# A recurrence and its experts on one core: experts in two walks, the first amid the recurrence's last third, weights in slices of 256 units, token rows scattered into slot order

## The chip, the cores and the metric

The kernel runs on one core of a Trainium2 chip. The metric is device time in microseconds (us) of one execution. The engines named below are TensorE (PE), VectorE (DVE), ScalarE (ACT), GpSimd (POOL) and SyncE (SP). PE's weight loads are shown apart (PEld). The clock in the views is the share of full TensorE clock that was granted.

## The reference

A linear recurrence runs over 768 steps for 4 x 8 heads of size 40. Its output, laid out as 3072 tokens of 320 numbers, goes through a mixture of eight experts: each token goes to the expert with the highest gate logit.

```python
for t in range(768):
    y[:, :, t] = einsum('bhd,bhde->bhe', r_t, state)
    Sa = einsum('bhde,bhe->bhd', state, a_t)
    state = state * w_t - einsum('bhd,bhe->bhde', Sa, b_t) + einsum('bhd,bhe->bhde', v_t, k_t)
x = y.transpose(0, 2, 1, 3).reshape(3072, 320)
e_idx = argmax(x @ w_gate); gate_w = softmax(x @ w_gate)[e_idx]
eom = sigmoid(x @ w_output_gate)
for e in range(8):
    h = maximum(x[e_idx == e] @ w1[e], 0)          # 320 -> 1024
    out[e_idx == e] = gate_w * eom[..., e] * (h @ w2[e])   # 1024 -> 320
```

All is float32. The routing must be exact enough to choose the same expert, and the products accurate, so each matmul operand of the experts is split into a high and a low part (hh and hl, w1h and w1l, and so on), and three products are summed.

## The kernel before

**The recurrence.** `Att` cuts the 768 steps into 12 chunks of 64 steps. A chunk has 16 pairs of heads in two halves (q = 0, 1); I call one (chunk, q) a half-chunk. For each chunk `scan` (POOL or DVE) makes running products of the decay w, `prep` makes the matrices LA, KB, WT and N from them (loads of D, PE products pl, ACT copies, POOL masks at L247, PE transposes at L159), and `tinv` inverts triangular 32 x 32 blocks on DVE (L276 to L317) for one or two chunks at a time. N goes through DRAM (Nd, Ns) to be laid out for `tinv`, and the inverse through Td to Tc. `crit` is the serial part of a half-chunk: pa (L370), solves with Tc (L380), a product with N (L407), another solve, XU (L417, L418), and the next state XS through pS (L427 to L437). `tail` makes the output x from it (pM at L463, pY at L480 and L481, x at L483).

`run` interleaves these by hand. The main loop goes through the half-chunks; after each step of `crit` it lets the tail of the half-chunk before take a step, lets the background take RATE = 4 steps, and the routing of finished halves one. The background is `prep` and `tinv` for all later chunks and, at its end, the early part of the experts. So that PE's clock stays up, `fill` issues dummy matmuls (L128, result fl, never read) at seven places of a half-chunk. The written order sets priorities; a scheduler with a timing model orders each engine's queue from it before the program runs, and on the chip each queue is in order.

**Routing.** `route` stores x to a DRAM array xd in token order (L631), transposes it, makes 16 logits (L642), and after chunks 3, 7, 10 and 11 calls `pick` for the chunks since the last pick. `pick` chooses the expert, counts slots (each expert has CAP = 480 of them, in four tiles of TS = 120), and scatters a record of four numbers for each token, namely row in xd, token, weight, and a spare, to a DRAM table tab in slot order (L714, one indirect DMA of 128 records for each half-chunk, 24 in all). Tokens of the first eight chunks (HALF = 7) stand in the first two tiles of each expert's slots (HT = 2), later ones behind, so that the first two can be worked on before the recurrence ends.

**The experts.** `weights` loads one expert's w1 and w2 in pieces of 4 KB rows (L738 to L748), ACT copies the high part, DVE subtracts for the low part. `tokens` gathers rows of xd for each tile through the table (L764, one indirect DMA of 120 rows each, 32 in all), transposes them on PE (L772) and splits them. `expert` makes eight hidden blocks of 128 units (eight matmuls each, L794; ACT relu L798; DVE low part L799) and then, tile by tile, the output po of 24 matmuls (L807 to L809), scaled on DVE (L811) and scattered to the output on POOL (L812). `early` loads expert 0's weights, waits for the pick of chunk 7, gathers two tiles of expert 0 and issues five of its eight hidden blocks (E0 = 5). All else is in `experts`, after the recurrence: experts 0 and 1 in halves of 240 rows, experts 2 to 7 with all 480 rows.

**Memory.** `Att` has a pool p0 (`s.p1`, one buffer a tile) that is closed when the last inverse is done; the early experts' pools take its place.

If an input is out of range or an expert overflows, a general version runs afterwards (`General`); it does not run here.

## Time and profile before

| what | us |
|---|---|
| median of three runs | 953.02 |
| the three runs | 936.96, 953.02, 960.29 |
| the profiled execution, its own time | 950.18 |
| its span, first to last instruction | 948.5 |
| mean granted clock in it | 0.818 |

Busy time over the span and the DMA traffic:

| engine or queue | busy us or MB |
|---|---|
| PE | 864.7 us (91%), 9226 matmuls |
| PEld | 720.2 us (76%) |
| DVE | 508.5 us (54%) |
| ACT | 352.0 us (37%) |
| POOL | 324.4 us (34%) |
| SP's and ACT's queues | 87.4 MB |
| POOL's queue | 8.9 MB |

Matmuls are pipelined, and a busy PE is not PE at its peak; the distance from one start to the next tells more. A line of the groups or the timeline names the source line, the engine, the operation, the tile written and the tiles read, then shapes, and how often. In the chain of waits, "issue" is time in which nothing that is recorded was waited for.

### The profile page before, as it was taken

To read this page: it belongs to the slowest core of one execution; us is meant where nothing else is said; L and a number is where in the kernel's file an instruction comes from. 1 tells how busy PE (TensorE), PEld (TensorE's weight loads), DVE (VectorE), ACT (ScalarE), POOL (GpSimd) and SP (SyncE) were. 2 spreads that over 40 slices of the span, in tenths; PEclk is the share of its full clock that TensorE was granted. 3 is DMA by queue.
4 is the path that set the end of the run, shared out by engine and by line. 5 is a ranking of instruction groups with operands and counts; after the bars stand their busy time and mean duration, and the time that the engine had idled before them with its cause. 6 is when DMAs were issued, how large, how long until landed. Compare 5 with 4: busy or idle time off the path is not lost.

```text
span 948.5 us, 22268 instructions
## 1 busy us (share of the span) xinstructions
PE 864.7 (91%) x9226; PEld 720.2 (76%) x9226; DVE 508.5 (54%) x1040; ACT 352.0 (37%) x835; POOL 324.4 (34%) x520
## 2 busy tenths in 40 slices
PE   6569699899999999999994999999899999999993
PEld 5457478788788788887873788888788788788873
DVE  8656948957944882388872321112535553544320
ACT  2566354754356135635211311111324542433110
POOL 7445567576255534502012000002252412231001
PEclk9555759999599669999876565556699999999997
DMA  8965277476266427535334321000655634351000
GB/s 187 187 124 116 60 164 157 99 178 136 74 145 131 100 77 177 109 81 125 80 81 73 86 49 35 24 24 13 162 146 157 180 116 119 87 162 55 11 14 23
DMA packets 151749, 97.77 MB, mean 103 GB/s; under 512 B 122678, under 2 KB 136825, under 8 KB 151642
## 3 DMA queue, kind: packets, MB, share of 16 engines
q1 hardware_dynamic: 146922, 87.30, 39.6%
q0 software_dynamic: 3840, 8.91, 3.3%
q8 instruction: 74, 1.21, 0.5%
q14 instruction: 33, 0.27, 0.1%
q10 hardware_dynamic: 880, 0.08, 0.1%
HBM read 73.48 MB, written 18.26 MB: 97 GB/s over the span
## 4 chain that ended last, share of the span: by engine, by line
PE 64%; DVE 14%; issue 8%; DMA 7%; POOL 3%; ACT 1%; SPq 0%; POOLq 0%; ACTq 0%; DVEq 0%
PE ph L794 14%; PE fl L128 7%; DVE tmpf L309 6%; PE pM L463 5%; PE po L809 5%; PE po L807 4%; PE po L808 4%; PE pa L380 3%; PE pl L241 3%; PE pa L370 2%; PE pS L427 2%; PE pY L481 2%; PE pxt L642 2%; PE pY L480 2%; DMA Nd<-N 2%
## 5 line engine op out<-in xcount | busy, mean ns | idle before, releaser
L247 POOL TENSOR_SCALAR_AFFINE_SELECT LA<-LA 64x192 f32<-64x192 f32 x144 | 62.4, 458 | 107.2 <-ACT LA L245 106.6
L714 POOL DMA_INDIRECT tab<-rec,si x24 | 25.1, 1045 | 211.7 <-DVE rec L711 174.3
L799 DVE SCALAR_TENSOR_TENSOR hl<-ph,hh 128x480 fp32r<-128x480 f32 (+1 forms) x75 | 41.8, 565 | 89.0 <-ACT hh L798 88.9
L794 PE MATMUL ph<-xl,w1h 128*128 128x480 f32 (+3 forms) x225 | 86.0, 383 | 0.0
L812 POOL DMA_INDIRECT out_dram<-y,ti x32 | 34.4, 1074 | 150.3 <-DVE y L811 90.3
L241 PE MATMUL pl<-Am,KBt 120*128 120x192 f32 (+1 forms) x288 | 71.7, 398 | 15.1 <-ACT Am L234 12.4
L794 PE MATMUL ph<-xh,w1h 128*128 128x480 f32 (+1 forms) x225 | 82.0, 366 | 0.6 <-DVE mem L692 0.3
L807 PE MATMUL po<-w2h,hh 128*120 128x320 f32 x256 | 80.2, 317 | 0.0
L808 PE MATMUL po<-w2l,hh 128*120 128x320 f32 x256 | 78.9, 312 | 0.0
L809 PE MATMUL po<-w2h,hl 128*120 128x320 f32 x256 | 78.4, 323 | 0.0
L798 ACT ACTIVATE hh<-ph 128x480 fp32r<-128x480 f32 (+1 forms) x75 | 36.6, 498 | 109.4 <-PE ph L794 109.4
L241 PEld LDWEIGHTS pl<-Am,KBt 120*128 120x128 f32 x288 | 57.0, 241 | 20.7 <-ACT Am L234 13.0
L463 PE MATMUL pM<-R,VU 104*128 104x128 f32 x384 | 71.4, 346 | 0.0
L118 POOL TENSOR_TENSOR Q<-Q,w 120x96 f32<-120x96 f32 x112 | 66.7, 634 | 0.1
L463 PEld LDWEIGHTS pM<-R,VU 104*128 104x128 f32 x384 | 61.7, 245 | 5.8 <-issue 2.3
L380 PE MATMUL pa<-As,Tc 32*32 32x40 f32 x1664 | 58.9, 224 | 6.2 <-ACT Tc L328 3.4
L469 DVE TENSOR_TENSOR M<-pM,mM 128x512 f32<-128x512 f32 x34 | 23.4, 689 | 74.6 <-PE pM L463 74.4
L481 PE MATMUL pY<-KB,M 128*64 128x40 f32 x768 | 62.1, 253 | 1.5 <-DVE M L469 1.2
L380 PEld LDWEIGHTS pa<-As,Tc 32*32 32x32 f32 x1664 | 46.7, 127 | 19.7 <-issue 7.0
L480 PE MATMUL pY<-Sd,R 104*64 104x40 f32 x704 | 60.2, 253 | 1.5 <-DVE M L469 1.5
L481 PEld LDWEIGHTS pY<-KB,M 128*64 128x64 f32 x768 | 54.5, 163 | 6.7 <-issue 4.0
L128 PE MATMUL fl<-As,zb 128*32 128x128 f32 x288 | 59.1, 338 | 0.0
(195 smaller groups left out, 1969.1 us busy)
## 6 DMA issues: line engine op xcount, KB each, us to landing
D<-in_din_dram SPq DMA_DIRECT2D x24, 540.0 KB
st<-in_w_dram SPq DMA_DIRECT2D x16, 512.0 KB
st<-in_w_dram SPq DMA_DIRECT2D x16, 480.0 KB
XS<-in_vt_dram SPq DMA_DIRECT2D x24, 256.0 KB
XU<-in_vt_dram SPq DMA_DIRECT2D x24, 256.0 KB
Nd<-N SPq DMA_DIRECT2D x24, 256.0 KB
VU<-in_vl_dram SPq DMA_DIRECT2D x24, 208.0 KB
w<-in_win_dram SPq DMA_DIRECT2D x12, 360.0 KB
```

What stands on the lines that cost most here:

```text
L118: g.tensor_tensor(out=run(m, z), in0=run(m - 1, z), in1=wr(m, z), op=ALU.mult)
L128: s.nc.tensor.matmul(s.fl[0:32, 0:src.free_size()], s.zb[0:src.partition_size()], src, start=True, stop=True)
L241: nc.tensor.matmul(pl[:, i, 0:nj], KBt[:, g0 + i].rearrange("p n t -> p (n t)"), Am[:, 0:nj, g0 + i], start=True, stop=True)
L247: g.affine_select(out=la[:, :, i], in_=la[:, :, i], pattern=[[0, nj], [1, C]], base=0, channel_multiplier=-1, compare_op=ALU.is_gt, fill=0.0)
L380: nc.tensor.matmul(pa[o:o + 32, i], Tc[o:o + 32, p, :], x[o:o + 32, i, :], start=True, stop=True, tile_position=(o, o))
L463: nc.tensor.matmul(pM[:, i], VU[:, h0 + i].rearrange("p n t -> p (n t)"), R[:, :, h0 + i], start=True, stop=True)
L480: nc.tensor.matmul(o, R[:, side, i, :], Sd[:, i, :], start=True, stop=False)
L481: nc.tensor.matmul(o, Ms[i // 4][:, i % 4, side, :], KB[:, side, p, :], start=not c, stop=True)
L794: nc.tensor.matmul(ph, l, r, start=(i == 0), stop=(i == 7))
L807: nc.tensor.matmul(po, hh[f][:, ts_], w2h[:, f], start=(f == 0), stop=False)
L808: nc.tensor.matmul(po, hh[f][:, ts_], w2l[:, f], start=False, stop=False)
L809: nc.tensor.matmul(po, hl[f][:, ts_], w2h[:, f], start=False, stop=(f == 7))
```

## The change

Experts are worked in two walks over all eight. Each walk takes two tiles (240 rows) of each expert: the first walk the tokens of chunks 0 to 7, the second those of chunks 8 to 11. The first is the end of the background and is written amid the recurrence's last third, with RATE2 = 3 steps for each step of `crit` and the dummy matmuls off (`hush`). The second comes after the recurrence. So every weight is loaded and split twice.

Weights come in slices of 256 hidden units (4 slices an expert, four DMAs each), three slices ahead in the first walk and six more in the second. A hidden block of one step is followed by the second matmuls of the block before it, for both tiles; these sum over all eight blocks in two banks. In the first walk the hidden result and the token transposes share one PSUM bank, the one that held the dummy matmuls' result; in the second, hidden results have three banks, transposes one and outputs four.

Token rows no longer go to xd. x stays on chip in a row of 324 numbers (six buffers) until its pick; then POOL writes token and weight into two of its columns, and the whole row of 322 numbers is scattered to a DRAM array slots in slot order. Eight DMAs of 622 KB on ACT's queue clear it beforehand. `fetch` loads 240 slots with one plain DMA on SP. There are seven picks instead of four, after chunks 1, 3, 5, 7, 9, 10 and 11.

To make room, KB and WT have four buffers instead of five, two scratch tiles and Tt move to the pool that is closed early, and `prep` of chunk c yields until the main loop has finished half-chunk (c - 3, 0).

```diff
+RATE2 = 3
+ROW = 324
     def fill(s, step, x):
-        s.warm(x, s.FILL[step])
+        if not s.quiet:
+            s.warm(x, s.FILL[step])
     def prep(s, c):
+        while s.fin < c - 4:
+            yield
-        KB = st['KB'] = s.p5.tile([128, 2, NP, 40], F32, name='KB', bufs=5)
+        KB = st['KB'] = s.p5.tile([128, 2, NP, 40], F32, name='KB', bufs=4)
     # tail
-        x = s.p2.tile([128, 8, 40], F32, name="x", bufs=2)
+        x = s.p2.tile([128, ROW], F32, name="x", bufs=6)
     # run
+                if c in (1, 2):
+                    for e in range(4 * c - 4, 4 * c):
+                        s.clear(e)
+                        yield
-                    adv(RATE)
+                    adv(RATE2 if s.quiet else RATE)
                 while next(tail, done) is not done:
                     pass
+                s.fin = c - 1 if q == 0 else s.fin
     # Moe
+    def clear(s, e):
+        s.nc.scalar.dma_start(out=s.slots[CAP * e:CAP * e + CAP].rearrange("(p n) f -> p n f", p=TS),
+                              in_=s.none.unsqueeze(1).broadcast_to([TS, CAP // TS, ROW]))
-    NB = {3: (0, 4), 7: (4, 4), 10: (8, 3), 11: (11, 1)}
+    NB = {1: (0, 2), 3: (2, 2), 5: (4, 2), 7: (6, 2), 9: (8, 2), 10: (10, 1), 11: (11, 1)}
     # route
-        nc.sync.dma_start(out=s.xd[256 * c + 128 * q:256 * c + 128 * q + 128], in_=xf)
+        s.X[2 * c + q] = xf = x
     # pick
-            nc.gpsimd.indirect_dma_start(out=s.tab, ..., in_=s.rec[:, 2 * c0 + i], ...)
+            x = s.X.pop(2 * c0 + i)
+            nc.gpsimd.tensor_copy(out=x[:, DM:DM + 2], in_=s.rec[:, 2 * c0 + i])
+            nc.gpsimd.indirect_dma_start(out=s.slots, ..., in_=x[:, 0:DM + 2], ...)
+    def load(s, e, g, p):
+        fs = slice(FS * g, FS * g + FS)
+        r1 = p.tile([128, 3, FS], F32, name="r1", tag="r1")
+        r2 = p.tile([128, 2, DM], F32, name="r2", tag="r2")
+        nc.sync.dma_start(out=r1[:, 0:2], in_=s.w1[e, 0:256, fs].rearrange("(k p) f -> p k f", p=128))
+        for h in range(2):
+            nc.sync.dma_start(out=r1[64 * h:64 * h + 64, 2], in_=s.w1[e, 256:320, fs])
+        nc.sync.dma_start(out=r2, in_=s.w2[e, fs].rearrange("(k p) f -> p k f", p=128))
+    def split1(s, r, p):
+        nc.scalar.copy(out=h, in_=r)
+        nc.vector.tensor_tensor(out=l, in0=r[:, 0:2], in1=h[:, 0:2].bitcast(F32), op=ALU.subtract)
+        nc.vector.tensor_tensor(out=h[64:128, 2], in0=r[64:128, 2], in1=h[64:128, 2].bitcast(F32), op=ALU.subtract)
...
+    def fetch(s, e, t0):
+        xg = s.tp.tile([TS, NT, ROW], F32, name="xg", tag="xg")
+        o = CAP * e + TS * t0
+        s.nc.sync.dma_start(out=xg, in_=s.slots[o:o + TS * NT].rearrange("(t p) f -> p t f", p=TS))
...
+    def walk(s, units, first, raw, ahead, wp, psx, ps1, ps2):
...
+        for u, (e, t0) in enumerate(units):
+            for g in range(4):
+                i = 4 * u + g
+                if more and g == 0:
+                    xg = s.fetch(*units[u + 1])
+                if more and g == 2:
+                    nt = s.turn(xg, psx)
+                    Tn = next(nt)
+                for fi in range(2):
+                    h = s.hidden(W[i], T, fi, ps1)
+                    yield
+                    if pend:
+                        s.second(*pend, ps2)
+                        yield
+                    pend = W[i], T, 2 * g + fi, h
+                    if i + 1 < len(sl):
+                        split(i + 1, fi)
+                    next(nt, None)
+                load(i + 1 + ahead)
...
+    def begin(s, ctx, psx, ps2, quiet):
+        s.raw, s.wp, s.tp, s.hp = pool("raw", LOOK), pool("wp", 2), pool("tp", 2), pool("hp", 4)
+        W = [s.load(0, g, s.raw) for g in range(LOOK)]
+        while not s.half:
+            yield
+        quiet()
+        yield from s.walk([(e, 0) for e in range(E)], W, s.raw, LOOK, s.wp, psx, psx, ps2)
+
+    def finish(s, ctx):
...
+        W = [s.load(0, g, s.raw) for g in range(LOOK)]
+        for _ in s.walk([(e, HT) for e in range(E)], W, pool("raw2", 6), 6, pool("wp2", 3), ps("px", 1), ps("ph", 3), ps("po", 4)):
+            pass
```

`turn` (not shown) transposes and splits the 240 rows as `tokens` did, `hidden` and `second` are the two halves of `expert`, `split2` splits w2 as `split1` does w1.

More of the change, by code (lines that the diff above doesn't have):

```diff
@@ L524, in background @@
             s.idle = True
-            if then:
-                yield from then()
+            yield from then()
         bg = background()
@@ L656, in pick @@
         n *= 2
-        mem = pool.tile([128, 8, 43], F32, name="mem", tag="mem", bufs=1)
+        mem = pool.tile([128, 4, 43], F32, name="mem", tag="mem", bufs=1)
         used = [0]
@@ L768, in tokens, with turn @@
+    def turn(s, xg, psx):
+        nc = s.nc
+        xh = s.tp.tile([128, 3, TS * NT], F32R, name="xh", tag="xh")
+        xl = s.tp.tile([128, 3, TS * NT], F32R, name="xl", tag="xl")
+        ti = s.tp.tile([TS, NT], I32, name="ti", tag="ti")
+        yield xh, xl, ti, xg
+        nc.vector.tensor_copy(out=ti, in_=xg[:, :, DM])
         for k in range(3):
             n = 128 if k < 2 else 64
-            pt = psx(TS * nt)
-            for t in range(nt):
+            pt = psx()[:, 0:TS * NT]
+            for t in range(NT):
@@ L778, in tokens, with hidden @@
             yield
[L780 removed]
+    def hidden(s, w, T, fi, ps1):
         nc = s.nc
[L783 to L814 removed]
@@ L816, in slots @@
-    def slots(s, pool):
-        nc = s.nc
-        tr = pool.tile([TS, 32, 4], F32, name="tr", tag="tr")
-        nc.sync.dma_start(out=tr, in_=s.tab.rearrange("(t p) f -> p t f", p=TS))
-        tb = pool.tile([TS, 4, 32], F32, name="tb", tag="tb")
-        nc.vector.tensor_copy(out=tb, in_=tr.rearrange("p t f -> p f t"))
-        ti = pool.tile([TS, 2, 32], I32, name="ti", tag="ti")
-        nc.vector.tensor_copy(out=ti, in_=tb[:, 0:2])
-        return tb, ti
-    def early(s, ctx, psx):
-        pool = lambda n, b: ctx.enter_context(s.tc.tile_pool(name=n, bufs=b, side="right"))
-        s.wpa, s.tp0 = pool("wpa", 1), pool("tp0", 1)
-        with s.tc.tile_pool(name="sp0", bufs=1, side="right") as sp:
-            w = s.weights(0, s.wpa, sp)
-            s.W0 = next(w)
-            yield from w
+        w1h, w1l = w[0:2]
@@ new lines, in hidden @@
+        xh, xl = T[0:2]
+        fs = slice(128 * fi, 128 * fi + 128)
+        ph = ps1()[:, 0:TS * NT]
+        seq = []
+        for k in range(2):
+            seq += [(w1h[:, k, fs], xh[:, k]), (w1h[:, k, fs], xl[:, k]), (w1l[:, k, fs], xh[:, k])]
+        seq += [(w1h[:, 2, fs], xh[:, 2]), (w1h[0:64, 2, fs], xl[0:64, 2])]
+        for i, (l, r) in enumerate(seq):
+            nc.tensor.matmul(ph, l, r, start=(i == 0), stop=(i == 7))
+        a = s.hp.tile([128, TS * NT], F32R, name="hh", tag="hh")
@@ new lines, in walk, with load, split @@
+    def walk(s, units, first, raw, ahead, wp, psx, ps1, ps2):
+        sl = [(e, g) for e, _ in units for g in range(4)]
+        R, W = dict(enumerate(first)), {}
+        def load(i):
+            if i < len(sl) and i not in R:
+                R[i] = s.load(*sl[i], raw)
+        def split(i, h):
+            W[i] = W.get(i, ()) + (s.split2 if h else s.split1)(R[i][h], wp)
+            if h:
+                del R[i]
+        xg = s.fetch(*units[0])
+        for i in range(ahead):
+            load(i)
+        yield
+        split(0, 0)
+        split(0, 1)
+        load(ahead)
+        t = s.turn(xg, psx)
+        T = next(t)
+        for _ in t:
+            yield
+        pend = None
+        for u, (e, t0) in enumerate(units):
+            more = u + 1 < len(units)
+            nt = iter(())
+            for g in range(4):
[16 more added lines that the diff above has]
+                load(i + 1 + ahead)
+            for _ in nt:
+                yield
+            if more:
+                T = Tn
+        s.second(*pend, ps2)
+        yield
```

211 lines of the change are left out of this document (66 added, 145 removed).

## The prediction

> **What bounds the kernel now.** I read the utilization slices of the page first. Each character is 23.7 us.
>
> ```profile
> PE   6569699899999999999994999999899999999993
> PEld 5457478788788788887873788888788788788873
> DVE  8656948957944882388872321112535553544320
> ACT  2566354754356135635211311111324542433110
> POOL 7445567576255534502012000002252412231001
> PEclk9555759999599669999876565556699999999997
> DMA  8965277476266427535334321000655634351000
> ```
>
> TensorE (PE) is full from slice 7 on, and no other engine is near full after slice 20. But from slice 21 to 28 its granted clock is 5 to 7 tenths: it is full at half speed. The expert stage (from slice 29) is full at full clock. The stretches of that part, by engine:
>
> ```profile
> 508.00:519.60 11.60, 0.00 (x0) 0.00 (x0) 0.47 (x2) 0.55 (x1) 3.08 (x3) 0.64 0.62 96
> 519.60:562.50 42.90, 42.89 (x414) 34.51 (x415) 12.97 (x25) 11.54 (x29) 0.00 (x0) 0.62 0.29 76
> 562.50:647.80 85.30, 84.46 (x923) 69.57 (x922) 13.62 (x38) 13.12 (x35) 2.04 (x2) 0.50 0.08 24
> 647.80:668.30 20.50, 16.70 (x196) 14.51 (x195) 4.70 (x18) 2.64 (x9) 3.92 (x4) 0.67 0.06 18
> 668.30:678.50 10.20, 10.20 (x37) 8.93 (x38) 4.53 (x15) 3.86 (x7) 4.63 (x4) 0.50 0.80 224
> 678.50:938.00 259.50, 253.89 (x1425) 212.39 (x1423) 114.48 (x174) 85.88 (x148) 67.05 (x59) 1.00 0.37 103
> 571.22:598.58 27.36, 27.36 (x292) 22.37 (x293) 4.18 (x9) 3.83 (x10) 0.00 (x0) 0.50 0.12 32
> ```
>
> Columns after the length: PE, weight load, DVE, ACT, POOL busy, clock, DMA share, GB/s. The recurrence's last third runs to 662 us, the experts from 668 to 933. In 562 to 648 PE is busy 84.46 of 85.30 us at clock 0.50. The last row is one half-chunk (from one XU copy to the next, 27.36 us). So two things are to be had: the expert work could run beside the recurrence, and its dense matmuls could lift the clock.
>
> The stretch before has this chain:
>
> ```profile
> 482.42 1.04 POOL tab L714
> ...
> 507.87 2.12 DMA tab<-rec,si
> 510.01 4.48 DMA tr<-tab
> 515.14 0.67 issue
> 516.06 3.51 DMA xg<-xd,ti
> ```
>
> Eight scatters of routing records, one after the other's landing, then the table, then two gathers. PE's queue had the token transposes ahead of the recurrence, so PE did nothing from 508 to 519.6 (first row above).
>
> **The change, step by step.** I sum up the changed kernel's span and compare it with this execution: span 948.5 us, time 950.18; the median of the three runs is 953.02, 0.3% above.
>
> Start of walk one. It needs the inverse of the last chunk done (its scratch is where the new pools go), a first weight slice, and 240 token rows of expert 0.
>
> ```profile
> 492.03 0.66 DVE L317 TENSOR_REDUCE Tt<-tmpf 64x64 f32<-64x512 f32 x1
> 499.26 1.22 DVE L744 TENSOR_TENSOR w1l<-st,w1h 128x1024 fp32r<-128x1024 f32 x1 [6.56 <-ACT w1h L742]
> ```
> ```profile
> out_dram<-y,ti POOLq DMA_INDIRECT x32, 3.1
> tab<-rec,si POOLq DMA_INDIRECT x24, 2.6
> ```
>
> The inverse ends at 492.7, and 6.6 us later the first weights are loaded and copied. The pick of chunks 6 and 7 now has four scatters instead of eight. Each carries a 1288-byte row instead of 16 bytes; the nearest row is the scatter of y (1280 bytes), 3.1 us to landing against 2.6. Spacing was (507.87 - 482.42) / 7.5 steps = 3.4 us; I take 3.6, so the last lands near 482.4 + 3 x 3.6 + 3.1 = 496. A plain load like the table's 4.5 us and 3 us of transposes and copies give 504. Bounds: 500 (weights alone) to 520 (as before).
>
> Ahead of that: the eight clears write 8 x 480 x 1296 bytes = 5.0 MB on ACT's queue. They cost nothing in a slice like the fifth (DMA 2 tenths), and up to 27 us (5.0 MB at the 187 GB/s that the first slices moved) if they all stand before the first loads; I take 4. The gate on prep and four KB buffers instead of five can start an inverse later; LA already rotates over four, so mostly the buffer waited before. 0 to 20 us; I take 4. Three more picks are some twenty small DVE operations each, off the path while PE is the full engine (0, at worst the same row as the gate's). Scatters of chunks 0 to 5 now stand on POOL earlier and in smaller lots, each waiting for the landing before it; behind them stand the scans (Q) and the masks of LA. The count is the same 24, 0.5 us longer to landing each, so up to 12 us of POOL, which the page shows at 5 to 7 tenths there: nothing on the path. Removing the 24 stores of x frees SP, and eight plain loads in each walk replace 32 gathers on POOL: worth nothing on the path beyond the start above. Start: 512.
>
> The price of the splitting operation on DVE, used below:
>
> ```profile
> L799 DVE SCALAR_TENSOR_TENSOR hl<-px,hh 128x240 fp32r<-128x240 f32 x5 | 1.9, 404 | 9.7 <-ACT hh L798 9.7
> ```
>
> Recurrence left at that point. From 519.6 to 662 is 142.7 us, of which 11 are five early hidden blocks; the rest over 27.36 is 4.8 half-chunks. The dummy matmuls, now silenced, are 6.96 us of each:
>
> ```profile
> 571.22:598.58 27.36, 6.96 (x27) 3.40 (x28) 0.50 0.12 32
> ```
> ```profile
> 280.57 1.10 PE pM L463 x8
> ...
> 589.53 2.01 PE pM L463 x8
> ```
>
> That leaves 20.4 us at half clock. The same eight pM matmuls take 1.10 us in a full-clock stretch against 2.01, so 0.55 to 0.57 of it: 11.6 us. 4.8 x 11.6 = 56 us.
>
> Walk one: eight units of 240 rows. Prices at full clock:
>
> ```profile
> 530.13 0.38 PE L794 MATMUL px<-xl,w1h 64*128 64x240 f32 x1
> 530.44 0.38 PE L794 MATMUL px<-xh,w1h 128*128 128x240 f32 x1
> ...
> 531.42 0.37 PE L794 MATMUL px<-xl,w1h 64*128 64x240 f32 x1
> ```
> ```profile
> 772.10 0.31 PE L807 MATMUL po<-w2h,hh 128*120 128x320 f32 x1
> ...
> 775.46 0.31 PE L809 MATMUL po<-w2h,hl 128*120 128x320 f32 x1
> ```
>
> A hidden block of eight takes 0.98 us to its last start and 0.31 more to the next: 1.29. The second matmuls step 3.36 / 23 = 0.146 us. A unit is 8 x 1.29 + 48 x 0.146 + six transposes (0.8) = 18.1 us; eight are 145.
>
> One bank (tag fl) holds both the hidden result and the transposes in this walk, so the next block waits for ACT's 0.37 and DVE's 0.40 us (row L799 above) plus handover. Beside the recurrence other matmuls fill that; 3.5 units remain after it (15 walk steps for each half-chunk, 16 a unit, so 4.5 go beside). There I add 8 x 0.3 and 3 x 1.3 us: 22 us. Bounds 0 to 45.
>
> Walk two: the same 145 us with three banks, plus 5 to change pools. What hides in it: weights are split again, per unit 4 x 1.8 us on DVE, hl 8 x 0.4, copies 2.3: 12.7 of 18.1, so DVE is not the bound. Weights come twice: 2.88 MB a unit, with rows in and out 3.5 MB in 18.1 us, 192 GB/s. DMA moved more than that in the present expert stage:
>
> ```profile
> 690.00:695.00 5.00, 5.00 (x35) 1.00 1.07 260
> ```
>
> That leaves a quarter spare. If the shorter runs (1 KB instead of 4) got only 187 GB/s, walk two would be 4 us longer. Fetches wait on SP for scatters; behind them stand weight slices (three ahead) and the loads of R, VU and XS. A pick late in the recurrence is 2 to 4 scatters, up to 15 us; three slices cover about 13 us of PE. I take 5 us, bounds 0 to 40.
>
> The tail is 933.1 to 948.5: 15 us, the same two last scatters.
>
> Sum at full clock: 512 + 56 + 145 + 22 + 5 + 145 + 5 + 15 = 905.
>
> **The clock** is what no row settles. Expert blocks begun cold need ten microseconds to lift it:
>
> ```profile
> 668.30 0.54 PE L794 MATMUL ph<-xh,w1h 128*128 128x240 f32 x1 [0.35 <-DVE mem L692]
> ...
> 670.55 0.57 PE L794 MATMUL ph<-xh,w1h 128*128 128x240 f32 x1
> ```
>
> A cold block is 2.25 us against 1.29, and the clock rose only at 678.5. Between 531 and 562, with 40 hidden matmuls among the recurrence, it stayed at 0.5 most of the time (0.62 on average). In walk one the expert share is larger, about 60% of PE's time. I take three cold spells of ten microseconds, each losing 43% (1 - 1/1.75): 13 to 15 us. Sum: 920 span, **922 us** in time.
>
> [...]
>
> **The rivals.**
> 1. The mixture stays cold (slower). Place: walk one beside the recurrence. For it: 0.62 from 519 to 562 with expert matmuls in the mix, and 0.50 for 85 us of full PE. Against it: the denser mix, and 400 to 467, where the recurrence beside prep held full clock. Price: 4.8 x (20.4 + 18.1 x 1.75) = 250 us instead of 4.8 x 29.7 = 143, so 905 + 107 = 1012, time 1014. It decides (over 972) once about 150 of those 250 us are cold.
> 2. Full clock throughout and the start as early as the sum has it without clears and gate: 905 - 8 = 897, less the 22 us of bank waits if the order covers some: 875 to 897, say 885. For it: 678 to 938 without a drop. Against: each wait for a scatter or a slice of over some microseconds (508 to 519.6) brings the clock down.
> 3. The order costs it: the gate makes inverses late, and in-order SP and PE queues stand behind fetches that wait for scatters, as at 508 to 519.6 (11.6 us once). Two or three such stalls and 20 us of the gate's bound: 920 + 30 = 950. No change.
>
> **How the numbers follow.** Forecast (895 to 940) 0.45, rival 1 0.20, rival 2 0.12, rival 3 0.23. The predicted time is the forecast's 922. The range runs from 880 (rival 2, most of it) to 990 (mixture cold for most of its length); about one in ten lies above, fewer below. A measurement of this kernel can tell about 2%: below 934 is faster, above 972 slower. Faster: 0.42 + 0.12 + 0.04 = 0.58. Slower: 0.20. Same: 0.22. The forecast's own range, cases of both signs being left in, is 895 to 940.
>
> **What would show it.** Walk one's first hidden block at 505 to 520; the clock row in 520 to 750 above 0.8; half-chunks (XU copy to XU copy) of about 30 us with a unit in each; units of 18 us in walk two at 1.00; last recurrence output near 660, walk two from about 755. Wrong: clock 0.5 through the mixture, idle PE before fetched rows, an XU series already late at 500, or DMA share near 1 with PE idle in walk two.

## The result, and the profile after

| kernel | median, us | range, us | runs |
|---|---|---|---|
| before | 956.65 | 936.96 to 961.5 | 4 |
| changed | 1038.61 | 1033.04 to 1052.28 | 4 |

The ratio is 1.100, with a 95% interval of 1.082 to 1.118; ratios in this text are of the faster executions of each kernel alone, so they differ a little from those of the medians. The changed kernel is slower by a tenth; the forecast was 922 us and faster. Its profiled execution took 1033.04 us, with a span of 1031.3 us and a mean granted clock of 0.802 (before: 948.5 us and 0.818).

The slices of the changed kernel's page (25.8 us each):

```profile
PE   5658789998998997799889999997888887999995
PEclk9555565699896788897976569997776899999998
DMA  8985253265526542463252722438533442566520
```

TensorE is less full at the start and again in slices 28 to 34, and in the first four of these the clock is 6 or 7 tenths. The last stretch, walk two, is full at full clock. Four stretches of the same trace (columns as in the forecast's first table: length; PE, weight load, DVE, ACT, POOL busy; clock; DMA share; GB/s):

```profile
157.50:521.10 363.60, 335.13 (x4808) 287.54 (x4809) 228.47 (x470) 154.52 (x404) 157.71 (x279) 0.81 0.45 103
583.70:669.70 86.00, 85.25 (x1066) 72.03 (x1065) 36.56 (x102) 31.04 (x75) 8.07 (x11) 0.85 0.41 111
725.70:868.50 142.80, 119.07 (x576) 93.41 (x576) 66.12 (x132) 50.29 (x98) 14.88 (x15) 0.82 0.41 120
893.00:1021.20 128.20, 124.63 (x802) 108.15 (x801) 81.45 (x171) 63.55 (x131) 14.00 (x14) 1.00 0.48 138
```

The first row goes from the second XU copy to the eighteenth, sixteen half-chunks. The second goes from the request for walk one's first rows to the last XU copy. It is mostly the mixture of recurrence and walk one, at a clock of 0.85 (0.96 from the first hidden block at 603.3 us on). The third is five units of walk one after the recurrence, from one unit's first output scatter to that of the fifth unit behind it: 142.8 / 5 = 28.6 us a unit, with TensorE idle for 23.7 us of it. The fourth is seven units of walk two: 128.2 / 7 = 18.3 us a unit.

Against the kernel before, stage by stage, in two traces of each kernel (the second ones are the runs g1_before and g2_after, further down):

| stage, us | before | changed |
|---|---|---|
| to the eighteenth XU copy | 467.9, 495.4 | 521.1, 509.2 |
| from there to the recurrence's last output | 194.9, 184.8 | 167.5, 183.0 |
| from there to the end | 285.7, 285.3 | 342.7, 342.2 |

```profile
662.80:948.50 285.70, 266.98 (x1473) 223.49 (x1473) 120.65 (x200) 90.66 (x158) 72.68 (x64) 0.95 0.37 102
```
```profile
688.60:1031.30 342.70, 297.43 (x1665) 245.73 (x1663) 178.04 (x381) 136.81 (x278) 35.42 (x36) 0.89 0.47 135
```

So most of what the changed kernel loses, 57 us in both pairs, lies behind the recurrence, in the units that are left there, although two units have been worked beside it. How far the start is behind differs between the pairs: 53 and 14 us.

Where the start went can be followed row by row in the timeline:

```profile
28.18 0.93 ACT L109 ACTIVATE sq<-w,wb 120x768 bf16<-120x768 f32 x1 [9.85 <-DMA slots<-none]
31.18 0.86 ACTq L638 DMA_DIRECT2D slots<-none  x1
117.61 0.42 ACT L425 COPY XU<-pa 64x320 f32<-64x320 f32 x1
157.50 0.42 ACT L425 COPY XU<-pa 64x320 f32<-64x320 f32 x1
521.11 0.42 ACT L425 COPY XU<-pa 64x320 f32<-64x320 f32 x1 [0.90 <-PE pa L388]
563.13 0.68 DVE L325 TENSOR_REDUCE Tt<-tmpf 64x64 f32<-64x512 f32 x1
563.83 0.49 SPq L329 DMA_DIRECT2D Td<-Tt  x1
575.92 0.37 SPq L333 DMA_DIRECT2D Tc<-Td  x1
583.66 0.41 SPq L779 DMA_DIRECT2D xg<-slots  x1
603.28 0.57 PE L814 MATMUL px<-xh,w1h 128*128 128x240 f32 x1
```

The scheduler has put all eight clears (L638) at the very start, from 10 to 32 us, and ACT stands behind their landing. The first XU copy comes at 117.6 us (88.6 before), the last inverse ends at 563.8 (492.7), the rows of the first unit are asked for at 583.7, and the first hidden block starts at 603.3 us, where the forecast had 512.

### The profile page after: what moved, and what is told of

Its sections match the earlier page's. It is cut to its first block, busy times and chain, and to the rows that moved or that the text cites. A ratio compares the mean times of both kernels' runs of the same rounds, so it can differ in the third digit from the quotient of the medians.

```text
span 1031.3 us, 23771 instructions
## 1 busy us (share of the span) xinstructions
PE 901.8 (87%) x9504; PEld 761.2 (74%) x9504; DVE 597.1 (58%) x1311; ACT 417.0 (40%) x998; POOL 294.1 (29%) x514
## 5 line engine op out<-in xcount | busy, mean ns | idle before, releaser
L839 POOL DMA_INDIRECT out_dram<-y,ti x32 | 32.9, 1027 | 328.4 <-DVE y L838 209.8
L831 PE MATMUL po<-w2h,hh 128*120 128x320 f32 x256 | 90.6, 360 | 10.9 <-ACT hh L817 7.9
L255 POOL TENSOR_SCALAR_AFFINE_SELECT LA<-LA 64x192 f32<-64x192 f32 x144 | 56.1, 413 | 94.6 <-ACT LA L253 94.1
L814 PE MATMUL px<-xh,w1h 128*128 128x240 f32 x192 | 63.9, 333 | 17.3 <-DVE hl L818 6.5
L249 PEld LDWEIGHTS pl<-Am,KBt 120*128 120x128 f32 x288 | 60.2, 252 | 18.3 <-ACT Am L242 9.6
L833 PE MATMUL po<-w2h,hl 128*120 128x320 f32 x256 | 71.6, 363 | 1.1 <-DVE hl L818 1.1
L817 ACT ACTIVATE hh<-px 128x240 fp32r<-128x240 f32 x64 | 23.8, 371 | 120.3 <-PE px L814 120.3
L489 PE MATMUL pY<-KB,M 128*64 128x40 f32 x768 | 60.2, 248 | 11.6 <-POOL M L480 11.6
L831 PEld LDWEIGHTS po<-w2h,hh 128*120 128x120 f32 x256 | 49.8, 195 | 25.5 <-ACT hh L817 21.7
L818 DVE SCALAR_TENSOR_TENSOR hl<-px,hh 128x240 fp32r<-128x240 f32 x64 | 25.9, 405 | 71.0 <-ACT hh L817 71.0
L814 PE MATMUL px<-xl,w1h 128*128 128x240 f32 (+1 forms) x192 | 66.8, 348 | 0.0
L814 PEld LDWEIGHTS px<-xh,w1h 128*128 128x128 f32 x192 | 43.1, 224 | 24.9 <-DVE xl L797 9.7
L378 PE MATMUL pa<-XS,LA 104*64 104x40 f32 (+1 forms) x768 | 45.7, 255 | 16.7 <-POOL LA L255 14.8
```

The lines of the kernel that those rows point to most:

```text
L249: nc.tensor.matmul(pl[:, i, 0:nj], KBt[:, g0 + i].rearrange("p n t -> p (n t)"), Am[:, 0:nj, g0 + i], start=True, stop=True)
L255: g.affine_select(out=la[:, :, i], in_=la[:, :, i], pattern=[[0, nj], [1, C]], base=0, channel_multiplier=-1, compare_op=ALU.is_gt, fill=0.0)
L378: nc.tensor.matmul(pa[64 * side:64 * side + 64, i], LA[0:kk, side, p, 0:64], XS[0:kk, side, i, :], start=(i == 0), stop=(i == 7), skip_gro ...
L489: nc.tensor.matmul(o, Ms[i // 4][:, i % 4, side, :], KB[:, side, p, :], start=not c, stop=True)
L814: nc.tensor.matmul(ph, l, r, start=(i == 0), stop=(i == 7))
L831: nc.tensor.matmul(po, a[:, ts_], w2h[:, f % 2], start=(f == 0), stop=False)
```

## The experiments

Medians stand beside the median of the kernel before on the same chip, which lay between 953 and 968 us.

### One bank for hidden blocks and transposes

e1_bank, and once more as h2_bank: after the recurrence, hidden blocks go to the two banks of tag pa, free by then; the transposes stay in fl.

```
-    ... walk(units, W, s.raw, LOOK, s.wp, psx, psx, ps2)
+    ... walk(units, W, s.raw, LOOK, s.wp, psx, ps1, ps2)
+    ps1 = lambda: ps([128, 512], "ph", "pa" if att.over else "fl", 2 if att.over else 1)()
```

> The changed kernel, but hidden blocks emitted after the recurrence's last output write the two banks of tag pa, which are then free; the transposes stay in fl. Theory (one bank for hidden blocks and transposes makes TensorE wait for the copies of each, and the short waits drop the clock): the units of walk one after the recurrence fall from about 30 us each (690 to 868 us for six) to 19 to 21, the clock in that stretch rises from about 0.75 to 0.95 or more, and the time falls by about 55 us, from 1038 to about 980. Rival (weight slices or fetched rows come late there, whatever the bank): units stay at 27 us or more, the time above 1020.

> The bank edit alone once more, on the same chip as the run before, since its four times lay between 977 and 1020. Theory (two separate costs): about 1000, level with the clears alone. Rival (the granted clock of the chip made the difference to the run with both): below 985 here.

Measured: 1003.84 us (977.01 to 1019.72; before 957.44), and 1010.55 us (989.98 to 1019.25; before 968.08). The same five units in the second of these runs:

```profile
717.50:824.80 107.30, 95.95 (x576) 81.36 (x575) 64.94 (x132) 49.48 (x98) 14.69 (x15) 0.95 0.55 160
```

The same 576 matmuls take 107.3 us instead of 142.8, at a clock of 0.95 instead of 0.82: 21.5 us a unit (21.0 in e1_bank). TensorE idles for 11.4 us instead of 23.7, so a third of the gain is waits and the rest is faster matmuls. So the bank cost the changed kernel some 35 us there, and 28 to 35 us of its time by the medians. The whole stage behind the recurrence's last output falls from 342.7 and 342.2 us to 307.3 and 308.5 (before: 285.7). The mechanism of e1_bank's theory holds, at less than its 55 us; its rival and that of h2_bank fall. How it does so is seen in the changed kernel's timeline of one hand-over (a transpose, its copies, the next hidden block) and in its waits from 690 to 868 us (total, times, longest):

```profile
774.36 0.37 PE L794 MATMUL px<-ident,xg 120*128 120x120 f32 x2
774.77 0.36 ACT L796 CAST xh<-px 128x240 fp32r<-128x240 f32 x1 [0.42 <-PE px L794]
775.56 0.41 DVE L797 TENSOR_TENSOR xl<-px,xh 128x240 fp32r<-128x240 f32 x1
776.02 0.49 PE L814 MATMUL px<-xh,w1h 128*128 128x240 f32 x1 [0.99 <-DVE xl L797]
```
```profile
PE po L831 <- ACT hh L817: 7.9, 16, 0.6
PE px L814 <- DVE xl L797: 6.5, 10, 1.0
PE px L814 <- DVE hl L818: 5.9, 5, 2.8
PE px L814 <- ACT xh L799: 4.3, 5, 1.0
```

Transposes finish at 774.8, but the next hidden block writes the same bank and has to wait until ACT and DVE have read it, to 776.0; DVE comes to its read only behind two weight splits (774.38 to 775.52). Each wait is under 1 us, save a few; with them the clock was 0.82, and 0.95 with the bank edit (more below).

### The clears

e5_clears: the clears alone, in the kernel before.

> The kernel before with the eight clears alone (5 MB of writes that nothing reads), issued where the changed kernel issues them. Theory (the clears stand ahead of the first loads): the first XU copy comes 25 to 30 us later than in the kernel before (88.6 us), at about 115 us, and the time rises by 15 to 29 us over 957. Rival (the delay is caught up, because the recurrence's early half waits for preparation anyway): first XU at 115 us, but the sixteenth XU copy (433.4 us in the kernel before) within 10 us of that, and the time within 8 us of 957.

Measured: 973.59 us (961.69 to 980.4), ratio 1.028 (1.017 to 1.040). The first XU copy is at 118.18 us, 29.6 late; the second at 153.50 is only 9.4 late (35.3 us between the two, 55.5 in the kernel before). The sixteenth, at 471.4, is 38 late, but how little that says is seen further down. The time rises by 20 us, as the theory had it, and the rival falls, though most of the first delay is regained at once. But span times mean clock is 773 to 786 us, within or next to the 762 to 785 of the kernel before (last section). So 9 us at the second XU copy are what the trace shows the clears to cost; the rest came with a lower granted clock, and that the clears brought this about isn't shown.

e2_late, h1_late3 and e12_bank_late: in the changed kernel the zeros come from a tile of chunk 0 (or 3), so that the scheduler can't put the clears ahead of it; the last of the three has the bank edit too.

```
-    if c in (1, 2):
-        for e in range(4 * c - 4, 4 * c):
+    if c == 3:
+        nc.gpsimd.tensor_scalar(out=none[:, 0:320], in0=s.st[3]["KB"][...], scalar1=0.0, op0=ALU.mult, ...)
+        for e in range(8):
             s.clear(e)
```

> The changed kernel, but the zeros that the eight clears write come from a tile of chunk 0, so that the clears can't start before chunk 0 is prepared. Theory (5 MB of clears at the very start delay the first loads): the first XU copy comes at about 90 us instead of 117.6, the recurrence's last output at about 665 instead of 688, the time falls by 20 to 29 us to about 1012. Rival (what is won at the start is lost again at the gate on the preparation): the first XU copy is early, but the last inverse still ends after 555 us and the time stays within 8 us of 1038.

> The changed kernel with the clears held back until chunk 3 is prepared, nothing else: the fourth corner beside the changed kernel (1038), the bank alone (1004) and both (964). Theory (the two costs are separate): about 1000, 35 to 40 us under the changed kernel. Rival (the clears cost 13 us at the second XU copy and the rest of what the run with both gained was the granted clock of that chip): 1020 to 1030.

> The changed kernel with the hidden blocks in the pa banks after the recurrence and the clears held back until chunk 3 is prepared, where the DMA share is below 0.5. Theory (the clears delay the start by 29 us and this lasts): the first XU copy comes at about 89 us, the second at about 145, the recurrence's last output at about 650, the time is 980 to 990. Rival (the start is regained anyway): the time within 8 us of 1004.

Behind chunk 0 (e2_late) nothing is won: 1055.74 us (1042.65 to 1068.98). The clears then run from 37 to 52 us, amid the loads of chunk 1, and the first XU copy is as late as before, 117.4 us, so neither the theory nor the rival comes true. Behind chunk 3, where they run from 117 to 135 us, the first XU copy is at 86.2 and 84.4 us and the time 1007.15 us (989.19 to 1039.75; before 968.08) without and 964.39 us (957.88 to 973.74; before 967.7) with the bank edit. From 1038.6 us, then, the clears' place alone is worth 31 us, the bank alone 28 to 35, and both 74: with both, the changed kernel is level with the kernel before, below the 980 to 990 that e12_bank_late's theory had. The lowest times give 44, 43 to 56 and 75 us, so whether the two gains add up isn't settled. They also differ in kind. The bank edit lowers span times clock by some 18 us; the clears' place leaves it where it was (816 to 835 us, against 824 to 835), so its gain is granted clock alone (0.786 to 0.839, against 0.784 to 0.807). h1_late3's median lies outside its rival's 1020 to 1030, but its four runs, 989 to 1040, take that in; that the chip made the difference isn't borne out, since the kernel before has a median of 968 beside both runs.

### The gate, the buffers and the picks

e3_gate (gate and four buffers), e9_picks (seven picks) and e10_gatepicks (both) in the kernel before; e6_all3 has the clears as well.

```
+        while s.fin < c - 4:
+            yield
-        KB = ... bufs=5        WT = ... bufs=5
+        KB = ... bufs=4        WT = ... bufs=4
-    NB = {3: (0, 4), 7: (4, 4), 10: (8, 3), 11: (11, 1)}
+    NB = {1: (0, 2), 3: (2, 2), 5: (4, 2), 7: (6, 2), 9: (8, 2), 10: (10, 1), 11: (11, 1)}
```

> The kernel before, with the gate on the preparation, four buffers of KB and WT instead of five, and the tiles Am2 and Nm in the single-buffer pool: that part of the change alone. Theory (the gate makes the inverses late): the last inverse ends at 525 us or later instead of 492.7, and the time rises by about 30 us, from 957 to about 985. Rival, the prediction's own view (LA's four buffers held the preparation back already): the last inverse ends before 500 and the time rises by at most 4 us.

> The kernel before with seven picks instead of four, nothing else. Theory (the gain of the run with clears, gate and picks came from the picks: four scatters instead of eight stand before the early experts' table and rows, so TensorE doesn't stop for 11.6 us and doesn't cool down there): TensorE idles at most 5 us ahead of the first hidden block, the time falls by 10 to 20 us to 937 to 947. Rival (it came from the gate, which moves preparation towards the recurrence's last third): time within 5 us of 955.

> The kernel before with the gate and the seven picks, without the clears. Theory (the clears cost what they cost alone, 2.8%, some 20 us): the time is about 916 to 925. Rival (the first half of the recurrence is bound by TensorE at its granted clock, so that most of a delay at the start comes back): 930 to 940, as with the clears.

> The kernel before with clears, gate (with its four buffers) and seven picks instead of four, the expert stage as it was. Theory (these three are what makes walk one's start late): the sixteenth XU copy at about 470 to 480 us (433.4 in the kernel before, 477.4 in the changed one) and the end of the last inverse at 555 to 570 (492.7 and 563.8). Rival (the scatters of whole rows, which this kernel has not, hold GpSimd and with it the preparation): the last inverse ends before 550, the sixteenth XU copy before 465.

In the changed kernel, each with something else changed beside the gate: e4_nogate has no gate and five buffers (and, for room, two raw slices and two y tiles); e7_three has the bank edit, the clears behind chunk 2, and the gate moved to the copies into KB and WT; e8_three5 is the same without any gate.

> The changed kernel without the gate, with five buffers of KB and WT again; to make room walk one holds two raw weight slices instead of three and two y tiles instead of three. Theory (the gate): the inverses stay behind those of the kernel before only by the 20 to 30 us of the start, the last one ends at about 520 to 535 instead of 563.8, walk one starts some 35 us earlier and the time falls by 20 to 40 us, to about 1008. Rival (the scatters on GpSimd's queue, each waiting for the landing before it, hold the masks and scans up): the last inverse still ends after 555 and the time stays above 1030.

> The changed kernel with the hidden blocks in the pa banks after the recurrence, the clears held back until chunk 2 is prepared, and the gate moved from the start of a chunk's preparation to the copies into KB and WT at its end. Theory (bank, clears and gate each cost what the first runs say): first XU at about 90 us, last inverse ends near 520, walk one starts near 535 and its units after the recurrence take 19 to 20 us; the time is about 945 to 960, 80 to 90 us under the changed kernel and level with the kernel before. Rival (moving the gate and the clears gives nothing, because the recurrence itself runs slower for lack of clock): last inverse after 540, the time about 985 to 1000, that of the bank alone.

> As the run before it, but without any gate and with five buffers of KB and WT (two raw slices and two y tiles in walk one). Theory: the last inverse ends near 510, and the time is about 940 to 960. Rival (two raw slices starve walk one): units of walk one beside the recurrence and after it above 22 us and weight copies that wait for their loads; the time above 980.

| run | us (range) | before there | eighteenth XU copy to end of last inverse, us |
|---|---|---|---|
| e3_gate | 967.62 (941.69 to 975.39) | 957.44 | 499.6 to 554.6: 55.0 |
| e9_picks | 972.73 (967.06 to 999.73) | 967.7 | 534.1 to 558.0: 23.9 |
| e10_gatepicks | 957.12 (945.22 to 964.15) | 967.7 | 517.4 to 563.9: 46.5 |
| e6_all3 | 936.13 (929.26 to 938.39) | 953.34 | 496.7 to 536.5: 39.8 |
| e4_nogate | 1044.72 (1023.32 to 1083.84) | 957.44 | 553.3 to 578.7: 25.4 |
| e7_three | 1008.12 (976.91 to 1049.62) | 953.34 | 531.8 to 540.0: 8.2 |
| e8_three5 | 1026.7 (1025.85 to 1031.91) | 953.34 | 529.8 to 554.9: 25.1 |

The last column is the gate's own mark. With the gate the last inverse ends 40 to 55 us after the eighteenth XU copy (42.7 in the changed kernel), without it 23 to 27 (24.8 in the kernel before, 26.8 in e5_clears), and with the gate moved 8.2. So the gate does hold the inverses back, by 15 to 30 us, 18 in the changed kernel. But neither taking it away nor moving it made the changed kernel faster: no run bears out a gain in time, and the theories of e4, e7 and e8 fall. (e8_three5 pays for its two raw slices: five units after the recurrence take 26.2 us each, where the bank edit with three slices has 21; its rival holds. e7_three's 540.0 and 1008 us lie next to its rival's numbers.) In the kernel before, gate and picks, alone or together, do not change the time by an amount that these runs tell. In e9_picks TensorE waits 1.9 us for the early expert's rows (12.6 and 13.1 in the two traces of the kernel before), about as its theory had it, but no time is gained; e10_gatepicks lies above its theory's range and its rival's.

The runs e6_all3 and e3_gate were to add up to the late start, and don't: in e6_all3 the sixteenth XU copy is at 460.4 and the last inverse ends at 536.5, the rival's numbers, in e3_gate the inverse is as late as the theory had it, but the time rises by 10 us, not 30.

e6_all3 is also a surprise: with clears, gate and picks the kernel before is a little faster, ratio 0.984 (0.976 to 0.993), though e5_clears is slower. It is the one version whose interval lies below the kernel before. Its clock is 0.819 to 0.846 where the kernel before had 0.793 to 0.829 on that chip; its span times clock, 767 to 785 us, is that of the kernel before. Why the clock was higher is not known.

### Was it the change, or the execution?

The eighteenth XU copy wanders from 467.9 to 553.3 us through these runs, with no order that clears, gate or picks explain. So both kernels were traced once more, unchanged.

> The kernel before once more, for a second trace. Theory (the last inverse's end at 492.7 us, on which the forecast's start of walk one rests, holds for the kernel): it ends within 10 us of that. Rival (the stretch from the second XU copy to the eighteenth, 324 us at a clock of about 0.88, is set by the granted clock of that execution): the stretch is longer where its clock is lower, so that length times clock stays between 285 and 300 us, and the last inverse ends between 490 and 545.

> The changed kernel once more, for a second trace. Theory (the late start of walk one is the change's own: clears and gate): the last inverse ends within 15 us of 563.8 and the stretch from the second to the eighteenth XU copy takes 355 to 370 us. Rival (mostly the granted clock of that execution): length times clock of that stretch stays between 285 and 300 us, at another length.

The stretch from the second to the eighteenth XU copy in five traces: the kernel before twice, the changed kernel's second, e9_picks, and e4_nogate (the changed kernel's first stands above).

```profile
144.10:467.90 323.80, 312.38 (x4787) 262.18 (x4788) 229.12 (x474) 154.60 (x405) 152.45 (x266) 0.91 0.53 120
```
```profile
141.20:495.40 354.20, 343.31 (x4785) 286.78 (x4785) 230.12 (x474) 154.98 (x405) 153.47 (x265) 0.81 0.49 109
```
```profile
155.70:509.20 353.50, 325.49 (x4808) 280.51 (x4809) 229.98 (x471) 155.12 (x404) 161.51 (x279) 0.83 0.47 107
```
```profile
147.80:534.10 386.30, 369.02 (x4795) 309.18 (x4795) 231.59 (x505) 156.41 (x410) 149.78 (x267) 0.75 0.45 100
```
```profile
154.70:553.30 398.60, 379.50 (x4827) 314.11 (x4828) 230.27 (x501) 155.00 (x403) 148.32 (x277) 0.73 0.40 94
```

Length times clock is 294.7, 286.9, 293.4, 289.7 and 291.0 us, and 294.5 in the changed kernel's first trace; over the traces of all 18 runs and the two first ones it lies between 287 and 304. The same 4,800 matmuls take 324 us at a clock of 0.91 and 399 at 0.73. So this stretch is bound by TensorE at whatever clock it is granted, in every kernel of the study, and the trace of before from which the forecast took its start of walk one had the highest clock of all. The second trace of the kernel before is 30 us longer there and ends its last inverse at 518.5 us instead of 492.7. The rival of g1_before holds. g2_after hardly separates its two: length times clock fits the rival, the last inverse at 551.0 us fits the theory, and the stretch of 353.5 us lies just under the theory's 355.

g1_before and g2_after ran this stretch at like clocks, 0.81 and 0.83, and took the same 354 us for it. So what the change itself puts on the last inverse is 551.0 - 518.5 = 32 us, 14 of them at the second XU copy and 19 at the gate, not the 71 us between the first two traces.

### The mixture, and the size of a unit

e11_nomix: with the bank edit, walk one begins only when the recurrence has ended. g4_nomix_late: the same with the clears behind chunk 3. g3_480: one walk of eight units of 480 rows, after the recurrence, clears behind chunk 3, dummy matmuls kept.

```
-        while not s.half:        (begin)
+        while not over():
...
-HT = NT = 2
+HT, NT = 0, 4                    (g3_480; no walk in begin)
```

> The changed kernel with the hidden blocks in the pa banks after the recurrence, but walk one begins only when the recurrence has ended; the dummy matmuls stay until then. Theory (the mixture pays: two units, some 36 us at full clock, ran beside the recurrence's last half-chunks at no price to these): the time is 25 to 40 us above that of the same kernel with the mixture (1004), about 1030 to 1045. Rival (the mixture pays nothing, since TensorE is busy in that stretch either way and the clock is what counts): within 12 us of 1004.

> Two walks of 240 rows, both after the recurrence, hidden blocks in the pa banks, clears held back until chunk 3 is prepared. Theory (the mixture saves nothing): within 12 us of the same kernel with the mixture (964). Rival (with the clears out of the way the mixture does pay): 985 or more.

> One walk of eight units of 480 rows after the recurrence instead of two walks of 240, with scattered rows and plain loads as in the change; clears held back until chunk 3 is prepared; dummy matmuls kept. Theory (units of 240 rows cost about 18.4 us each, 36.8 a pair, where 480 rows at once cost the 31.1 us between two experts in the kernel before): the experts take 8 x 31 to 33 us, the last output of the recurrence comes at about 650, the time is about 930 to 950, at or below the kernel before. Rival (a unit is bound by its weight splits on DVE and ACT, not by TensorE): 36 us an expert or more, the time above 970.

Measured: e11_nomix 991.33 us (974.15 to 997.09) against 1003.84 and 1010.55 with the mixture; g4_nomix_late 970.04 us (964.9 to 978.54) against 964.39. The mixture pays nothing that these runs can tell; the theory of e11 falls, that of g4 holds. Without it the recurrence takes 138 to 152 us from the eighteenth XU copy to its last output (e11, g4, g3), with two units beside it 162 to 183 (the changed kernel's two traces, e1, h2, h1, e12), so most of the two units' 36 us is paid there. The last half-chunks show why. The rows are four half-chunks of the kernel before, and five of g4_nomix_late, with the same dummies:

```profile
546.00:640.20 94.20, 93.62 (x1080) 77.08 (x1080) 14.33 (x34) 14.84 (x41) 0.00 (x0) 0.54 0.13 33
```
```profile
527.40:614.50 87.10, 84.63 (x1357) 71.77 (x1357) 32.19 (x76) 21.47 (x55) 7.72 (x10) 0.79 0.36 91
```

23.6 us a half-chunk at a clock of 0.54, and 17.4 at 0.79. (In e11_nomix and g3_480 the clock of the same five half-chunks is 0.82 and 0.77, in g1_before that of the last four 0.62.) The cold last third, which the mixture was to warm, is no fixture of the recurrence. That the dummy matmuls keep the clock up is what they were written for; no run here takes them out alone. Nor do the five early hidden blocks of the kernel before bring it about by themselves. e9_picks has them there too, and its last four half-chunks took 61.6 us:

```profile
601.50:663.10 61.60, 61.02 (x1097) 52.15 (x1097) 20.26 (x59) 17.88 (x49) 4.12 (x4) 0.96 0.26 68
```

And the mixture does not always warm it. From the first hidden block to the last XU copy the clock is 0.96 and 0.76 in the changed kernel's two traces, 0.60 in e2_late and 1.00 in h1_late3. In e7_three, with both in the queue, TensorE was busy without a gap and the clock stayed at half:

```profile
600.00:650.00 50.00, 50.00 (x447) 42.07 (x447) 14.66 (x30) 11.50 (x27) 0.00 (x0) 0.51 0.19 52
```

g3_480 took 955.03 us (947.8 to 966.22; before 960.94), ratio 1.002 (0.996 to 1.008), 15 us below g4_nomix_late and just above its theory's 930 to 950. Two first scatters that are five experts apart, in g3_480 and in the kernel before:

```profile
733.80 1.00 POOL L841 DMA_INDIRECT out_dram<-y,ti  x1 [18.48 <-DVE y L840]
...
899.40 1.00 POOL L841 DMA_INDIRECT out_dram<-y,ti  x1 [18.92 <-DVE y L840]
```
```profile
767.91 1.03 POOL L812 DMA_INDIRECT out_dram<-y,ti  x1 [13.54 <-DVE y L811]
...
927.54 0.99 POOL L812 DMA_INDIRECT out_dram<-y,ti  x1 [19.31 <-DVE y L811]
```

That is 33.1 and 31.9 us an expert. Two units of 240 rows take 2 x 18.3 = 36.6. So the small unit costs 3.5 us an expert against g3_480, 28 over eight. (The 14 units that are left behind the recurrence are 14 x 18.3 = 256 us, eight experts of the kernel before 8 x 31.9 = 255: the two units beside the recurrence only make up there for the smaller size.) g3_480 gives part of that back, since its first unit can't start before the last scatters. The level of the kernel before is reached, not beaten.

## Why the forecast was wrong, point by point

| part of the span, us | forecast | trace | difference |
|---|---|---|---|
| to walk one's first hidden block | 512 | 603.3 | +91 |
| from there to walk one's last unit (868.5) | 56 + 145 + 22 + 15 = 238 | 265.2 | +27 |
| the rest | 5 + 145 + 5 + 15 = 170 | 162.8 | -7 |
| span | 920 | 1031.3 | +111 |

**The start (+91)** is the step that failed. It sums up from four shifts, less the 8 us that the forecast had allowed for clears and gate:
- Second XU copy: 157.5 - 144.1 = 13. The clears were taken as 4 of a bounded 27. The forecast placed them where the DMA queues had room; no data that they need holds them there, and the scheduler put them first.
- Sixteen half-chunks: 363.6 - 323.8 = 40. This is granted clock, and 30 of it the second trace of the kernel before shows too. The forecast took a moment out of one execution for a property of the kernel.
- Eighteenth XU copy to last inverse: 42.7 - 24.8 = 18. The gate, "mostly the buffer waited before", was taken as 4 of 20; the table of seven runs sets it near the upper bound or above.
- Last inverse to first hidden block: 39.5 instead of 492.7 to 504, 11.3, so 28. The fetch stands on SP behind XS, Tc and R, which wait for the recurrence for some 8 us (2.5, 4.3 and 1.6), and behind the issuing of weight slices (563.8 to 583.7); the transposes and copies stand in PE, ACT and DVE queues that are full of recurrence at a clock of 0.50 (583.7 to 603.3, TensorE busy for 19.40 of 19.6 us). The forecast counted these operations with their durations alone. The kernel before takes 33.9 and 32.9 us for the same way in its two traces, and the forecast put that down to its eight scatters; here the four scatters were done 20 us ahead of the last inverse. The third rival had the gate and the in-order queues, but with the recurrence behind the fetch; here the fetch stood behind the recurrence.

**Walk one after the recurrence (+27).** The mechanism was right, the size wrong: bank waits of 22 us for 3.5 units, 6.3 a unit. Since the start was late, six units were left instead of 3.5, and each took 28.6 us where the forecast's unit with waits was 24.4. The bank edit shows that 7 of the 10 us over walk two's 18.3 were the bank and the clock it cost: 21.5 us a unit without it. (The 27 is net: about three half-chunks were left at the late start instead of 4.8, some 20 us less by the forecast's price.) With bank and clears mended (e12_bank_late) the time is 964 us; the 42 that still lack to 922 weren't taken apart.

**The mixture.** Beside the recurrence the clock was 0.96 in the first trace, above the 0.8 that the forecast asked for, but 0.76 in the second, so that the first rival did not come true in the one and did for a part in the other. e2_late and e7_three show more of it; e7_three has the widest spread of the study (976.91 to 1049.62). But the gain that the forecast took from the mixture, 4.8 half-chunks at 11.6 us instead of 27.4, rested on the recurrence being cold without it. In e11, g4, g3 and e9 it was not, or much less so, and in e11 and g4 the mixture was worth nothing. This step was wrong in its premise, again read from one execution.

**Right:** walk two's unit (18.1 forecast, 18.3 measured) at full clock with DMA at half its share (1.00 and 0.48); the seven picks cost nothing that shows (e9_picks, 972.7 against 967.7; whole-row scatters were not run alone, but g3_480 has them and is level with the kernel before); the tail (10 us instead of 15). The late scatters of chunks 10 and 11, at 730 to 743 us, hurt nothing, since walk two begins at 868.

**What stays open:** why the granted clock of one kernel differs between executions; whether the clears' place brings the higher clock by which h1_late3 is 31 us faster, when the second XU copy moves by only 9 (157.5 to 148.5); and why the clock of e6_all3 is above that of the kernel before.

## What to carry to other kernels

A moment in one trace (an inverse's end, a cold stretch) is a sample where TensorE is the bound and its clock changes (the last inverse of the kernel before ended at 492.7 us at a clock of 0.91, and at 518.5 at 0.81): trace the unchanged kernel twice before a sum rests on it. Transposes and the products that use them did better here in banks of their own: 21.5 us a unit at a clock of 0.95, against 28.6 at 0.82 in one bank, where most waits were under a microsecond. A store that nothing waits for goes where the scheduler likes; give it an operand from the stage beside which it is to run (chunk 3 here, which brought the first XU copy from 117.6 to 86.2 us; chunk 0 was too early to help).

## What the runs showed of the hardware

**The clock fell behind windows in which TensorE was partly busy, and not every busy window brought it back.** Cut end to end into 299 windows of 3.413 us, from 8.2 to 1028.8 us, the changed kernel's trace has a clock of 0.50 or 0.51, or of 0.99 or 1.00, in each of them and nothing between; so in this trace the clock changed at their borders. Some of those behind the recurrence:

```profile
731.83:735.24 3.41, 3.41 (x21) 2.57 (x19) 0.75 (x2) 1.38 (x3) 1.71 (x2) 1.00 0.83 233
735.24:738.66 3.42, 1.40 (x9) 1.00 (x8) 2.13 (x5) 0.81 (x2) 0.92 (x2) 0.99 0.22 81
738.66:742.07 3.41, 2.85 (x11) 1.94 (x9) 0.66 (x2) 0.49 (x2) 1.12 (x1) 0.50 0.80 246
...
755.72:759.13 3.41, 2.94 (x10) 2.13 (x10) 1.31 (x4) 1.10 (x2) 0.46 (x1) 0.50 0.29 96
759.13:762.55 3.42, 3.42 (x14) 2.88 (x14) 0.91 (x3) 0.57 (x2) 0.56 (x1) 0.51 0.69 179
762.55:765.96 3.41, 3.38 (x23) 2.86 (x23) 2.08 (x5) 1.62 (x3) 1.01 (x1) 1.00 0.34 103
...
772.79:776.20 3.41, 1.96 (x12) 1.44 (x11) 2.17 (x5) 2.11 (x4) 0.00 (x0) 0.99 0.25 84
776.20:779.61 3.41, 2.95 (x11) 2.46 (x12) 0.90 (x2) 0.37 (x1) 0.00 (x0) 0.50 0.68 195
...
803.50:806.92 3.42, 2.20 (x14) 1.61 (x13) 1.75 (x4) 2.11 (x4) 0.00 (x0) 1.00 0.37 96
806.92:810.33 3.41, 2.70 (x16) 2.09 (x16) 1.32 (x3) 0.65 (x2) 0.00 (x0) 1.00 0.57 147
...
871.71:875.12 3.41, 2.83 (x16) 1.90 (x14) 0.40 (x1) 1.84 (x5) 1.00 (x1) 1.00 0.14 35
875.12:878.53 3.41, 3.40 (x14) 2.98 (x13) 2.53 (x7) 0.85 (x3) 0.00 (x0) 0.50 0.05 15
```

After a window with TensorE busy for 1.40 or 1.96 us the clock was at half; after one with 2.20 it stayed. At half clock, windows with 2.85 to 2.95 us busy did not lift it, one with 3.42 did. Between 690 and 868 us the clock fell five times, each time behind a window with TensorE busy for 1.40 to 1.98 us (41 to 58%), and stayed at half for 7 to 24 us (two to seven windows). So here 1.4 to 2.0 us of waits in one window were followed by several windows at half clock. Busy time alone does not settle it: the last two rows show a window with 2.83 us busy behind which the clock was at half, for one window; at half clock, one with 3.06 (711.35 to 714.77) was followed by full clock and others with 3.05 to 3.19 (704.53, 813.74, 817.16) were not. In e7_three TensorE was busy without a gap in fourteen such windows in a row (600.0 to 647.8 us), and the clock was 0.50 in every one. In the kernel before, with TensorE idle before the fetched rows, the clock was 0.98 in the first 3.40 us (508.0 to 511.4) and 0.50 in the next. What else counts, no run here took apart.

**Time times clock belongs to the kernel.** Span times mean clock, the length that a span has when it is counted in full-speed time, spreads much less than the time. In 42 executions of the kernel before, beside five groups of experiments, the time ran from 927.85 to 978.69 us, this product only from 762 to 785.

| kernel | span times clock, us |
|---|---|
| before (42 executions) | 762 to 785 |
| before, with clears; gate; picks; gate and picks; all three | 773 to 786; 770 to 790; 769 to 775; 779 to 781; 767 to 785 |
| changed (5 executions, 1033 to 1052 us) | 824 to 835 |
| clears behind chunk 3 (h1_late3) | 816 to 835 |
| bank edit (e1_bank, h2_bank) | 805 to 818 |
| both (e12_bank_late) | 813 to 822 |
| both, no mixture (g4_nomix_late) | 811 to 818 |
| one walk of 480 rows (g3_480) | 779 to 793 |

Where the times are blurred by the clock, this tells the edits apart. Clears, gate and picks leave the product about where it was. The change adds some 55 us to it; the bank edit takes 12 to 18 off, and one walk of 480 rows some 29 more than g4_nomix_late. What it can't tell is why one kernel is granted more clock than another.
